# A fused attention and gated feed-forward kernel: another order for the first stretch, and the 1/rms of batches 2 to 7 by TensorE transposes

## The chip, the core and the metric

The kernel runs on one core of a Trainium2 chip. A core has engines that run side by side, each with its own queue of instructions: TensorE multiplies matrices (PE in the profile; PEld are its loads of the stationary operand), VectorE (DVE), ScalarE (ACT) and GpSimd (POOL) work on elements, and SyncE (SP) issues transfers. Results of TensorE go to PSUM, the other engines work on SBUF and PSUM. Engines wait for each other by semaphores. The metric is the device time of the whole kernel in microseconds (us).

## What is computed

Eight batches of 512 tokens with 8 heads of 64 features, and 32 states per head. Tokens read the states and states read the tokens by softmax attention; both results, 544 rows of 512 features per batch, go through an RMS norm and a gated feed-forward layer with 1536 hidden features.

```
scores  = x @ state.T / 8                    # per batch and head: 512 x 32
xread   = softmax(scores)  @ state           # tokens read states
sread   = softmax(scores2) @ x               # scores2 = state @ x.T / 8
rows    = concat(xread, sread), heads side by side      # (8*544, 512)
xn      = rows / sqrt(mean(rows^2) + 1e-6) * rms_g
out     = (silu(xn @ w_gate) * (xn @ w_val)) @ w_out    # 1536 hidden
```

The inputs w_gate, w_val, w_out come as 64-bit numbers and are converted on the chip.

## The kernel before

The kernel is a set of streams, Python generators that issue a few instructions and yield. A string of letters names the stream that goes on next; so it deals the order of instructions on TensorE, VectorE and ScalarE by hand, while GpSimd and the transfers follow the program. ORDER deals batch 0, the conversion of weights and the attention of batch 1; PERIOD deals one batch b from 1 to 7 with the attention of batch b+1; STATES deals the feed-forward layer of the states at the end.

```python
streams = {"a": tokens_read(0), "s": states_read(0), "A": tokens_read(1), "S": states_read(1),
           "e": exponents(), "d": values(),          # conversion: ScalarE's part, VectorE's part
           "v": ...own_weights(0, mp)...,            # state @ w, and its copies
           "h": of_batch_0(0), "t": of_batch_0(1), "u": of_batch_0(2),   # products, silu, gates
           "p": project_as_ready(banks_0), "c": projected(banks_0, store_tokens(0)),
           "w": first_of_batch(1), "k": weight_sums(), "z": keep_awake()}
with tc.manual_schedule(**by_hand):
    for stream in ORDER:
        if stream in "ck" and "s" not in seven:
            early.close()          # the room of raw weights is given back
            open_late()            # and the pools of the later batches are opened
            slot_sums(1)
        next(streams[stream])
...
for b in range(1, B):
    ...
    h, t, u = hidden_seven(S, weights_of(b), lambda b=b: tokens_of(b), False)
    p, c, k = project_seven(S, store_tokens(b))
    ...                            # "a" tokens_read(b + 1), "s" states_read(b + 1),
    ...                            # "w" first_products(b + 1, then); in the last batch
    ...                            # "a" is state_norm() and sums_of_w([0]), one step in four
    for stream in PERIOD:
        if stream in streams:
            step = next(streams[stream], done)
```

keep_awake (z) multiplies the identity by itself and its result is not used. From batch 1 on, products of two by two blocks are done with seven multiplications in place of eight: slot_sums makes sums of the attention weights (L610 to L613, GpSimd), more_of_v sums of the weights (L572 to L575, GpSimd), hidden_seven the products (L692) and gates, project_seven the projection (L854).

Attention of the tokens, with the norm (one yield is one step of the stream):

```python
def mean_root(ss, n):                      # L271: ss ** -0.5 on GpSimd
    ri = two.tile([P, NC], F32, name="ri")
    GE.tensor_tensor(out=ri[:, 0:n], in0=ss, in1=mhalf[:, 0:n], op=ALU.pow)
    return ri

def along_rows(ri, n):                     # L278: each column along all rows, to PSUM
    rp = aps.tile([P, NC, P], F32, name="at")
    for c in range(n):
        TE.transpose(out=rp[:, c, :], in_=ri[:, c:c + 1].to_broadcast([P, P]), identity=ident)
    return rp.rearrange("p c t -> p (c t)")

def rms_on_array(b, sq):                   # batches 0 and 1
    ...                                    # L348: four products with a column of ones
    VE.tensor_scalar(ss, sp, 1e-6, None, op0=ALU.add)
    yield "step"
    ri = mean_root(ss, NC)
    yield
    rp = along_rows(ri, NC)
    yield
    return rp

def rms_on_blocks(b, sq):                  # batches 2 to 7
    n = S // Ns                            # 16
    VE.transpose(out=sq[:, 1, :], in_=sq[:, 0, :])                       # L364
    yield
    part = one.tile([P, n], F32, name="part")
    VE.reduce_sum(out=part, in_=sq[:, 1, :]..., axis=AXX)                # L367
    yield
    sp = aps.tile([P, n], F32, name="at")
    TE.matmul(out=sp, lhsT=groups..., rhs=part, start=True, stop=True)   # L370
    yield
    ss = two.tile([P, n], F32, name="ssb")
    VE.tensor_scalar(ss, sp, 1e-6, None, op0=ALU.add)                    # L374
    yield "step"
    ri = two.tile([P, n], F32, name="rib")
    GE.tensor_tensor(out=ri, in0=ss, in1=mhalf, op=ALU.pow)              # L377
    yield
    rp = sq[:, 2, :]
    VE.transpose(out=rp, in_=ri.unsqueeze(2).to_broadcast([P, n, Ns]))   # L380
    yield
    return rp

def tokens_read(b):
    ...                                    # scores (L328), max, exp, sums (L337 to L412)
    VE.transpose(out=aT_s[b][:, e], in_=eS[:, e]...)                     # L414
    ...
    TE.matmul(out=reads[j]..., lhsT=packed..., rhs=aT_s[b]...)           # L421
    ...
    SE.activation(out=sq[:, i, :], in_=reads[j], func=ACTF.Square, ...)  # L428
    ...
    VE.tensor_tensor(out=sq[:, i, :], ..., op=ALU.add)                   # L431
    ...
    rp = yield from (rms_on_array if b < 2 else rms_on_blocks)(b, sq)
    VE.tensor_tensor(out=aT_s[b], in0=aT_s[b], in1=rp..., op=ALU.mult)   # L434
    yield "step"
```

Attention of the states: L447 and L450 (maximum), L454 (exponentials), then for batches 0 and 1 L464 (transposes on TensorE) and L466 (copies), for the others L472 (eB, transpose on VectorE), L475 (eB to e_d in DRAM) and L479 (e_d to e2T); L482 and L483 (sums), L490 (products with x), L498, L502, L504 (the result into xsT).

Conversion of one piece of the weights: L216, L218, L221 on ScalarE, then L242, L245, L249, L254 on VectorE. L546 is the product of states and weights, L588 the hidden product of batch 0, L598 its gates, L794 its projection. The gates of the later batches are L754, L757 and L769 on VectorE, copies L738, L741, L743 and the activation L745 on ScalarE.

The norm of the states, in the last batch:

```python
def state_norm():
    ...                                                            # L510: squares on ScalarE
    yield
    ...                                                            # L515: products with ones
    ss = two.tile([P, NT // P], F32, name="sst")
    VE.tensor_scalar(ss, sp, 1e-6, None, op0=ALU.add)              # L518
    ri = mean_root(ss, NT // P)
    yield
    rp = along_rows(ri, NT // P)
    for i in range(NI):
        VE.scalar_tensor_tensor(out=xsT[:, i, :], ...)             # L523
    sums_of_x()
    yield
```

Of the kernel before, what the change touches and what calls it, by code (L numbers as in the profile page):

```python
# [8 lines left out]
F32 = mybir.dt.float32  # L9
# [3 lines left out]
ALU = mybir.AluOpType  # L13
# [4 lines left out]
P = 128  # L18
# [1 line left out]
W_BUFS = 3  # L20

ORDER = (
    "aaaaaaaaddaaaaaaeaseeaasadsasszzzzzzzzzzzzzzssdsaaaasaeadesaeeazzsdasaaezzzzzzza"
    "deadaaaddeeazzzzsedaadszzzzzadaeedzzvvavdzzadeaAzzzzhdeeddtdAdAAhueheAeedtddphAe"
    "dvdvduvdphedeAedtdhApeehddeuAdddeAhdedvdtudvvpeAAAAdhdAAteAehuhpddephepdeAdAeApA"
    "dteedAAvvveAdpudAAephtdSdhAdphdeAueedhAdeAteudddeeSppAddAAdppAdAdevApvdveehhAdth"
    "AudhpdeddeedeAdteAupvdvdvphedAAtdShhutSAhpukSSSkkkwSwkpSkpwpSSckSScckkpcSwkkkwww"
    "w"
)

PERIOD = (
    "hhvthtaxhxthauhvuvthhtauhthxhaahtuuxxuxahuhuatthtuuhxhhuutuxhuhthhuhuttauhxthhhu"
    "ahuuuavhattuhtxuhhxhutuuauuthaaauhaxhhthtutuhuhuhuuuaptuuuhupuacpaaaaaaaapaaaapa"
    "kacaakapssaaaaaspcsspakcakkcaaucksaawwsxwxppxksssxppskkpsxskpcxsscs"
)

STATES = (
# [6 lines left out]
def kernel(  # L44
# [21 lines left out]
    VE, SE, GE, TE = nc.vector, nc.scalar, nc.gpsimd, nc.tensor  # L66

    B, H, S, D = x.shape
    Ns = state.shape[2]
    DM = H * D  # L70
    DFF = moe_w_gate.shape[1]
    NC = S // P
# [7 lines left out]
    consts = ctx.enter_context(tc.tile_pool(name="consts", bufs=1))  # L80
    one = ctx.enter_context(tc.tile_pool(name="one", bufs=1))
    two = ctx.enter_context(tc.tile_pool(name="two", bufs=2))
# [8 lines left out]
    seven = {}  # L91
# [17 lines left out]
    def load_x(b, *queues):  # L109
# [8 lines left out]
        for c in range(NC):  # L118
# [3 lines left out]

    ident = consts.tile([P, P], F32, name="ident")
    make_identity(nc, ident)
    mhalf = consts.tile([P, S // Ns], F32, name="mhalf")
    GE.memset(mhalf, -0.5)
    ones = consts.tile([P, 1], F32, name="ones")
    GE.memset(ones, 1.0)

    GE.tensor_tensor(out=consts.tile([P, NC], F32, name="first_pow"), in1=mhalf[:, 0:NC],  # L130
                     in0=ones.to_broadcast([P, NC]), op=ALU.pow)
    bounds = consts.tile([P, 2], F32, name="bounds")
    GE.memset(bounds[:, 0:1], 1151.0 + 7.5 / 16)
# [4 lines left out]
    for i in range(4):  # L138
        GE.tensor_copy(groups[:, i], ident[:, 0:Ns])
        for j in range(1, 4):  # L140
            GE.tensor_tensor(out=groups[:, i], in0=groups[:, i],
                             in1=ident[:, Ns * j:Ns * j + Ns], op=ALU.add)
# [125 lines left out]
    def mean_root(ss, n):  # L268
# [5 lines that stand above are left out]
    def along_rows(ri, n):  # L274
# [5 lines that stand above are left out]
# [80 lines left out]
    def rms_on_blocks(b, sq):  # L360


        n = S // Ns
# [3 lines that stand above are left out]
        VE.reduce_sum(out=part, in_=sq[:, 1, :].rearrange("p (k f) -> p k f", f=Ns), axis=AXX)  # L367
        yield
        sp = aps.tile([P, n], F32, name="at")
        TE.matmul(out=sp, lhsT=groups.rearrange("p i t -> p (i t)"), rhs=part,  # L370
                  start=True, stop=True)
        yield
        ss = two.tile([P, n], F32, name="ssb")
        VE.tensor_scalar(ss, sp, 1e-6, None, op0=ALU.add)  # L374
        yield "step"
        ri = two.tile([P, n], F32, name="rib")
        GE.tensor_tensor(out=ri, in0=ss, in1=mhalf, op=ALU.pow)  # L377
        yield
        rp = sq[:, 2, :]
        VE.transpose(out=rp, in_=ri.unsqueeze(2).to_broadcast([P, n, Ns]))  # L380
        yield
        return rp

# [123 lines left out]
    def state_norm():  # L507

        sq = one.tile([P, NI, NT], F32, name="sqT", tag="eS")
        SE.activation(out=sq, in_=xsT, func=ACTF.Square, scale=DM ** -0.5)  # L510
        yield
        sp = aps.tile([P, NT // P], F32, name="at")
        for r in range(NT // P):
            for i in range(NI):
                TE.matmul(out=sp[:, r:r + 1], lhsT=sq[:, i, P * r:P * r + P], rhs=ones,  # L515
                          start=(i == 0), stop=(i == NI - 1))
        ss = two.tile([P, NT // P], F32, name="sst")
        VE.tensor_scalar(ss, sp, 1e-6, None, op0=ALU.add)  # L518
        ri = mean_root(ss, NT // P)
        yield  # L520
        rp = along_rows(ri, NT // P)
        for i in range(NI):
            VE.scalar_tensor_tensor(out=xsT[:, i, :], in0=xsT[:, i, :], scalar=rms_g[:, i:i + 1],  # L523
                                    in1=rp[:, 0:NT], op0=ALU.mult, op1=ALU.mult)
        sums_of_x()
        yield
# [7 lines left out]
    def own_weights(b, mp):  # L534


        pv = []

        def products():
            w = w_sb.pop(b * (NM // 2) + mp)  # L540
            for e in range(2):
                pv.append(vps.tile([P, 4 * P], F32, name="pv") if b and mp % 2 == 0 else
                          aps.tile([P, 4 * P], F32, name="at"))
            for j in range(4):
                for e in range(2):
                    TE.matmul(out=pv[e][Ns * j:Ns * j + Ns, :],  # L546
                              lhsT=stT_g[b][D * e:D * e + D, j, :],
                              rhs=w[D * e:D * e + D, j].rearrange("p m k f -> p (m k f)"),
                              start=True, stop=True)
            fetch(b * (NM // 2) + mp + W_BUFS)  # L550
            yield

        def copies():
            v = (seven["v"] if b else v_0).tile([P, 2, 2, 2, P], F32, name="v")
            v_sb[b, mp] = v, None
            for e in range(2):
                SE.copy(v[:, e].rearrange("p m k f -> p (m k f)"), pv[e])  # L557
                yield
            if b:
                more_of_v(b, mp)  # L560
                yield

        return products(), copies()
# [42 lines left out]
    def slot_sums(b):  # L606

        tt = aT_t[b] = seven["late"].tile([P, 3, HS], F32, name="aT_t")
        b11, b12, b21, b22 = (aT_s[b][:, e, HS * i:HS * i + HS] for e in range(2) for i in range(2))
        GE.tensor_tensor(out=tt[:, 0], in0=b12, in1=b11, op=ALU.subtract)  # L610
        GE.tensor_tensor(out=tt[:, 1], in0=b22, in1=tt[:, 0], op=ALU.subtract)
        GE.tensor_tensor(out=tt[:, 2], in0=b21, in1=tt[:, 1], op=ALU.subtract)
        GE.tensor_tensor(out=b12, in0=b22, in1=b12, op=ALU.subtract)  # L613
# [56 lines left out]
    def sums_of_x():  # L670

        tt = seven["late"].tile([P, 3, HI, P], F32, name="x_t")
        b11, b12, b21, b22 = blocks_of_x()
        x_sums.extend(tt[:, i] for i in range(3))
        for to, a, b in ((tt[:, 0], b12, b11), (tt[:, 1], b22, tt[:, 0]), (tt[:, 2], b21, tt[:, 1]),
                         (b12, b22, b12)):
            VE.tensor_tensor(out=to, in0=a, in1=b, op=ALU.subtract)
# [138 lines left out]
    def open_late():  # L816
        seven["late"] = ctx.enter_context(tc.tile_pool(name="late", bufs=1))
        seven["v"] = ctx.enter_context(tc.tile_pool(name="vbufs", bufs=3))
        seven["vs"] = ctx.enter_context(tc.tile_pool(name="sums", bufs=3))
        seven["c22"] = ctx.enter_context(tc.tile_pool(name="late2", bufs=2))  # L820
        seven["pool"] = ctx.enter_context(tc.tile_pool(name="halves", bufs=7))
        seven["t"] = seven["late"].tile([P, 3, HM, HD], F32, name="wt")
        seven["s"] = seven["late"].tile([P, HM, HS], F32, name="hs")
# [123 lines left out]
            yield  # L947

    def first_of_batch(b):
        for mp in range(2):  # L950
            for part in own_weights(b, mp):
                yield from part

    def first_products(b, own):
        slot_sums(b)
        yield
        for part in own:
            yield from part[0]
# [15 lines left out]
    for k in range(1, RAW_AHEAD):  # L974
# [6 lines left out]
               "h": of_batch_0(0), "t": of_batch_0(1), "u": of_batch_0(2),  # L981
               "p": project_as_ready(banks_0), "c": projected(banks_0, store_tokens(0)),
               "w": first_of_batch(1), "k": weight_sums(), "z": keep_awake()}
    by_hand = dict(engines={mybir.EngineType.PE, mybir.EngineType.DVE,
                            mybir.EngineType.Activation})
    with tc.manual_schedule(**by_hand):
        for stream in ORDER:
            if stream in "ck" and "s" not in seven:
                early.close()
                open_late()  # L990
                slot_sums(1)
            next(streams[stream])
    assert all(next(stream, done) is done for name, stream in streams.items() if name != "z")
    load_state(2)
# [2 lines left out]
    for b in range(1, B):  # L997
# [11 lines left out]
        if b + 1 < B:  # L1009
            streams.update(a=tokens_read(b + 1), s=states_read(b + 1),  # L1010
                           w=first_products(b + 1, then))
# [9 lines left out]
    n = B * (NM // 2)  # L1021
# [37 lines left out]
```

## Time and profile before

| | before |
|---|---|
| time, median of 3 | 789.96 us (788.03 to 791.89) |
| span of the profiled run | 786.2 us, granted clock 0.998 |
| PE busy | 764.7 us |
| DVE busy | 540.6 us |
| ACT busy | 325.0 us |
| POOL busy | 179.6 us |

The page of a profile gives busy times of each engine, the span in 40 slices with the busy share in tenths, the chain of work that ended last, and groups of instructions by line. Further views give the waits (engine and line, for whom, us in total, times, longest), and the timeline (start in us, duration in us, engine, line, operation, output<-inputs, count; in brackets the idle time before it and who ended it). A multiplication of this kernel's 32-bit numbers shows as two records of PE, a transpose as one. The end of a PE record is modelled and overlaps the start of the next, so durations of PE add up to more than its time.

The stretches of the span: the first stretch to about 134 us, batches 1 to 7 of about 84 us each but the last, in which no attention is left, and the states' layer, whose first products begin at 711 us among the last of batch 7.

### The profile page before, as it was taken

The numbers are of one execution on the slowest core, as the hardware profiler recorded it, in microseconds if no ns is written. First come the engines' busy times: TensorE is split into PE (matmuls) and PEld (weight loads), VectorE is DVE, ScalarE is ACT, GpSimd is POOL, SyncE is SP. The second block draws the span as 40 slices with busy tenths as digits, with TensorE's granted clock in tenths as the row PEclk, the third lists the DMA queues.
The fourth block names the chain that finished last, engine by engine and source line by source line (L and its number), as shares of the span: only waits on it lengthen the run. The fifth ranks groups of instructions, "written<-read, shape, count | busy, mean of one in ns | idle before, by whom it ended". The sixth has DMA issues, their size and how long they took to land.

```text
span 786.2 us, 12078 instructions
## 1 busy us (share of the span) xinstructions
PE 764.7 (97%) x4698; PEld 583.2 (74%) x4698; DVE 540.6 (69%) x834; ACT 325.0 (41%) x536; POOL 179.6 (23%) x232
## 2 busy tenths in 40 slices
PE   6999999999999998999999999999999997999998
PEld 5643444778868876877877877788788775888997
DVE  4999997688548971888278845895379715862461
ACT  5998874652235322543154224522353223510320
POOL 2100003430424024310542052304331152300000
PEclk9999999999999999999999999999999999999999
DMA  9778864760457034720665065704451253101310
GB/s 295 222 274 311 277 188 157 253 181 3 177 167 248 1 103 151 261 80 18 207 211 158 5 201 163 226 1 161 145 188 44 75 171 130 54 1 41 122 55 27
DMA packets 73689, 112.98 MB, mean 144 GB/s; under 512 B 40865, under 2 KB 51617, under 8 KB 66721
## 3 DMA queue, kind: packets, MB, share of 16 engines
q1 hardware_dynamic: 60512, 92.75, 35.5%
q10 hardware_dynamic: 13120, 19.47, 8.4%
q8 instruction: 37, 0.61, 0.3%
q14 instruction: 20, 0.16, 0.1%
HBM read 87.56 MB, written 24.64 MB: 143 GB/s over the span
## 4 chain that ended last, share of the span: by engine, by line
PE 82%; DMA 8%; DVE 8%; issue 1%; ACTq 1%; ACT 0%; SPq 0%
PE f L692 37%; PE f L854 27%; DMA e_d<-eB 5%; PE f L794 5%; PE pv L588 4%; PE at L546 3%; DMA e2T<-e_d 2%; PE pv L546 2%; PE at L328 1%; DVE ex L249 1%; PE at L490 1%; PE at L421 1%; DVE raw L245 1%; ACTq L479 1%; DVE eB L472 1%
## 5 line engine op out<-in xcount | busy, mean ns | idle before, releaser
L854 PE MATMUL f<-wo,hb 128*128 128x256 f32 x540 | 123.9, 382 | 0.0
L692 PE MATMUL f<-aT_s,v 128*128 128x256 f32 x504 | 120.7, 382 | 1.0 <-DVE hb L769 1.0
L854 PEld LDWEIGHTS f<-wo,hb 128*128 128x128 f32 x540 | 101.5, 190 | 23.1 <-issue 9.9
L692 PEld LDWEIGHTS f<-aT_s,v 128*128 128x128 f32 x504 | 94.0, 190 | 24.7 <-issue 12.4
L692 PE MATMUL f<-aT_t,vs 128*128 128x256 f32 x336 | 87.8, 384 | 0.0
L754 DVE TENSOR_TENSOR g<-g,f 128x512 f32<-128x512 f32 (+1 forms) x96 | 61.3, 651 | 33.9 <-PE f L692 26.1
L745 ACT ACTIVATE hb<-g 128x1024 f32<-128x1024 f32 (+1 forms) x48 | 48.2, 1004 | 86.5 <-DVE g L754 86.5
L854 PE MATMUL f<-wt,hs 128*128 128x256 f32 x360 | 80.4, 379 | 0.0
L692 PEld LDWEIGHTS f<-aT_t,vs 128*128 128x128 f32 x336 | 62.6, 190 | 20.4 <-issue 11.7
L572 POOL TENSOR_TENSOR vs<-v 128x256 f32<-128x256 f32 x42 | 32.8, 780 | 188.2 <-ACT v L557 188.2
L854 PEld LDWEIGHTS f<-wt,hs 128*128 128x128 f32 x360 | 68.3, 190 | 9.4 <-issue 0.2
L891 ACT COPY ot<-f 128x256 f32<-128x256 f32 x60 | 20.8, 374 | 129.1 <-PE f L854 129.1
L377 POOL TENSOR_TENSOR rib<-ssb,mhalf 128x16 f32<-128x16 f32 x6 | 19.7, 3289 | 177.2 <-DVE ssb L374 177.2
L757 DVE SCALAR_TENSOR_TENSOR hb<-hb,g 128x1024 f32<-128x1024 f32 x42 | 54.8, 1305 | 5.1 <-ACT hb L745 5.1
L899 DVE TENSOR_TENSOR ot<-ot,f 128x256 f32<-128x256 f32 x45 | 17.4, 414 | 58.7 <-PE f L854 54.3
L557 ACT COPY v<-at 128x512 f32<-128x512 f32 x54 | 29.1, 593 | 56.0 <-POOL vs L575 31.1
L692 PE MATMUL f<-aT_t,v 128*128 128x256 f32 x168 | 43.3, 380 | 3.1 <-DVE c L754 3.1
L794 PE MATMUL f<-wo,hb 128*128 128x512 f32 x96 | 44.7, 600 | 0.0
L588 PE MATMUL pv<-aT_s,v 128*128 128x512 f32 x96 | 43.6, 593 | 0.0
L692 PE MATMUL f<-aT_s,vs 128*128 128x256 f32 x168 | 43.1, 379 | 0.0
L854 PE MATMUL f<-wt,hb 128*128 128x256 f32 x180 | 41.8, 383 | 0.0
L743 ACT COPY g<-f 128x512 f32<-128x512 f32 (+1 forms) x48 | 27.0, 562 | 34.3 <-PE f L692 34.3
(145 smaller groups left out, 1255.5 us busy)
## 6 DMA issues: line engine op xcount, KB each, us to landing
w_m<-w_d SPq DMA_DIRECT2D x48, 1024.0 KB, 5.4
out_dram<-ot SPq DMA_DIRECT2D x56, 128.0 KB, 1.8
raw<-in_moe_w_val_dram SPq DMA_DIRECT2D x6, 1024.0 KB, 5.2
raw<-in_moe_w_out_dram SPq DMA_DIRECT2D x6, 1024.0 KB, 7.8
x_b<-in_x_dram SPq DMA_DIRECT2D x96, 64.0 KB, 2.4
w_d<-w_m SPq DMA_DIRECT2D x6, 1024.0 KB, 4.9
x_d<-xB ACTq DMA_DIRECT2D x6, 1024.0 KB, 7.9
xG<-x_d ACTq DMA_DIRECT2D x24, 256.0 KB, 4.9
```

Source lines behind the costliest of these rows:

```text
L546: TE.matmul(out=pv[e][Ns * j:Ns * j + Ns, :], lhsT=stT_g[b][D * e:D * e + D, j, :], rhs=w[D * e:D * e + D, j].rearrange("p m k f -> p (m k ...
L557: SE.copy(v[:, e].rearrange("p m k f -> p (m k f)"), pv[e])
L572: GE.tensor_tensor(out=vs[:, 0], in0=a21, in1=a22, op=ALU.add)
L588: TE.matmul(out=to[0], lhsT=lhs(i, k), rhs=r, start=(i == 0), stop=(i == len(rhs) - 1))
L692: TE.matmul(out=ps[:, i, 0:half], lhsT=l[:, i, :], rhs=r, start=(start and i == 0 and k == 0), stop=(k == len(lhs) - 1), skip_group_check= ...
L743: SE.copy(gates(q)[1], q["x"][:, :, 0:half])
L745: SE.activation(out=hb[:, 2 * mp:2 * mp + 2, 0:n].rearrange("p m (c t) -> p m c t", c=2), in_=q["g"][:, :, :, 0:half], func=ACTF.Silu if s ...
L754: VE.tensor_tensor(out=to, in0=to, in1=q[ps][:, :, 0:half], op=ALU.add)
L757: VE.scalar_tensor_tensor(out=h, in0=h, scalar=1.0, op0=ALU.add, op1=ALU.mult, in1=q["g"].rearrange("p m c t -> p m (c t)"))
L794: TE.matmul(out=banks[r], lhsT=hb[:, m, P * r:P * r + P], rhs=wo[:, m, :], start=(m == 0), stop=(m == NM - 1))
L854: TE.matmul(out=banks[name][:, r, :], lhsT=lhs(k)[:, P * r:P * r + P], rhs=rhs(k), start=(start and r == 0 and k == 0), stop=(k == HM - 1) ...
L891: SE.copy(to, banks[name][:, r, :])
```

## The change

Four things differ. ORDER is dealt anew, by a longer search. The slot sums of batch 1 become the first step of stream w, which now may be the one that opens the later pools, so they come after the change of room. In batches 2 to 7 the row of 1/rms comes by a power of 4 columns and four transposes on TensorE, as in batches 0 and 1, and no longer by a power of 16 columns and a transpose on VectorE; PERIOD is dealt for that. The norm of the states gets two more yields. It is meant to fill the first stretch better. Line numbers after the change are two or three higher than before (L588 becomes L590, L692 L694, L546 L548).

```diff
 ORDER = (
-    "aaaaaaaaddaaaaaaeaseeaasadsasszzzzzzzzzzzzzzssdsaaaasaeadesaeeazzsdasaaezzzzzzza"
-    "deadaaaddeeazzzzsedaadszzzzzadaeedzzvvavdzzadeaAzzzzhdeeddtdAdAAhueheAeedtddphAe"
     ... (four more lines cut)
+    "aaaaaadaaaaadeeaaeaaeadaaaeeaaaeaaadaadeaaeadddzzzzzzzzzzzzzzzzzzzzzzzzaaadaddee"
+    "daaaeazzzzzzzzzzzvvzaddeadvazzzAeeadeaedzzzhtdddAehAuAhdAeAeeAAtdpdddedpddvvvhue"
     ... (four more lines cut)
 )
 PERIOD = (
     ... (its three lines are replaced; the counts of each letter stay)
 )
@@
-    mhalf = consts.tile([P, S // Ns], F32, name="mhalf")
+    mhalf = consts.tile([P, NC], F32, name="mhalf")
@@ rms_on_blocks
-        ss = two.tile([P, n], F32, name="ssb")
-        VE.tensor_scalar(ss, sp, 1e-6, None, op0=ALU.add)
+        ss = two.tile([P, NC], F32, name="ss")
+        for g in range(4):
+            VE.tensor_scalar(ss[Ns * g:Ns * g + Ns], sp[Ns * g:Ns * g + Ns, g::4], 1e-6, None,
+                             op0=ALU.add)
         yield "step"
-        ri = two.tile([P, n], F32, name="rib")
-        GE.tensor_tensor(out=ri, in0=ss, in1=mhalf, op=ALU.pow)
-        yield
-        rp = sq[:, 2, :]
-        VE.transpose(out=rp, in_=ri.unsqueeze(2).to_broadcast([P, n, Ns]))
+        ri = mean_root(ss, NC)
+        yield
+        rp = along_rows(ri, NC)
         yield
         return rp
@@ state_norm
                 TE.matmul(out=sp[:, r:r + 1], lhsT=sq[:, i, P * r:P * r + P], rhs=ones,
                           start=(i == 0), stop=(i == NI - 1))
+        yield
         ss = two.tile([P, NT // P], F32, name="sst")
         VE.tensor_scalar(ss, sp, 1e-6, None, op0=ALU.add)
         ri = mean_root(ss, NT // P)
         yield
         rp = along_rows(ri, NT // P)
+        yield
         for i in range(NI):
@@ first_of_batch
+        slot_sums(b)
+        yield
         for mp in range(2):
@@
-            if stream in "ck" and "s" not in seven:
+            if stream in "ckw" and "s" not in seven:
                 early.close()
                 open_late()
-                slot_sums(1)
             next(streams[stream])
```

Letters in ORDER: z goes from 40 to 42, w from 8 to 9, all others keep their counts. In the old ORDER stream s (batch 0's states) runs early, between the fillers z; in the new one it comes while batch 0's products run.

## The prediction

> **What bounds the kernel now.** I read the page first, then the waits, then the timeline of single engines.
>
> ```profile
> PE 764.7 (97%) x4698; PEld 583.2 (74%) x4698; DVE 540.6 (69%) x834; ACT 325.0 (41%) x536; POOL 179.6 (23%) x232
> ...
> PE   6999999999999998999999999999999997999998
> DVE  4999997688548971888278845895379715862461
> ...
> PE 82%; DMA 8%; DVE 8%; issue 1%; ACTq 1%; ACT 0%; SPq 0%
> ```
>
> PE is the bound nearly everywhere, so the kernel gets shorter only where PE gets less to do or waits less. What the 97% hides is seen in start times: in steady work a 128x256 record starts 0.216 us after the one before it (four L692 records take 0.86 us), though its mean duration is 382 ns. So I count PE's work from start to start.
>
> Three places are not full of useful work. First, the start:
>
> ```profile
> 11.23 6.31 PE L945 MATMUL f<-ident 128*128 128x256 f32 x28
> 17.38 1.04 PE L464 MATMUL at<-ident,e 128*128 128x128 f32 x8
> ...
> 19.21 1.10 PE L490 MATMUL at<-x_b,e2T 128*32 128x64 f32 x64
> 20.24 3.29 PE L945 MATMUL f<-ident 128*128 128x256 f32 x14
> ...
> 38.48 1.88 PE L588 MATMUL pv<-aT_s,v 128*128 128x512 f32 x4
> ```
>
> L945 multiplies the identity only to keep PE busy. The real products begin at 38.48, once DVE has scaled batch 0's weights (L434, 36.84 to 38.06). Second and third, the waits of PE and one of DVE:
>
> ```profile
> PE at L490 <- DMA e2T<-e_d: 5.2, 5, 2.0
> ...
> PE f L692 <- DVE c L754: 3.1, 1, 3.1
> ...
> DVE sst L518 <- PE at L515: 7.9, 1, 7.9
> ```
>
> In six batches PE waits for the transfer of e2T; the start times give 1.29, 2.17, 0.35, 1.05, 0.89 and 0.60 us lost, 6.35 us in all. (The view counts less because the modelled end of the matmul before reaches into the gap.) The other two belong to one event in the last batch: DVE stands 7.9 us at L518, where the norm of the states waits for PE, and the gates behind it come late. Start to start PE loses 0.46 us at L515, then 1.13 and 3.23 us: 4.8 us.
>
> **What the Trainium skill says.** "TensorE: Matmul & The Clock Gate", section "Step-by-step: what each phase is for": matmuls stay in program order, only weight loads are pulled ahead. So a matmul placed before its data is ready stops all behind it; the trace agrees, the 3.07 us wait for L754 is followed by products that were ready. Same page, "Part 4: PE-mode transpose": a full 128x128 transpose, to PSUM only, about 275 ns in a kernel. The trace has 278 ns for L278, but 109 ns from start to start, which is what I charge. "DMA: Bandwidth & Descriptors", "Anatomy of one DMA": about 2 us are fixed, mostly the receipt of the last write. The trace has 3.0 us for 128 KB of e2T and 7.8 us for the 512 KB of e_d, so there something more than the fixed part is paid. "ScalarE: Activation LUTs", "What ACT_TABLE_LOAD costs": 1283 ns for a load plus a drain; the trace has 1283 ns for each of its six loads.
>
> **The change, part by part**, with the instruction order of the changed kernel (built, not run) beside this trace.
>
> *Start.* The new order takes batch 0's states (stream s) out of the start; the tokens and the conversions before L434 stay. Off DVE's queue go L447 twice (0.61 and 0.59 us to the next start), L450 (0.07), L482 (0.20), L483 (0.09), L498 twice (0.30), L504 (0.20): 2.06 us. L434 also waited 0.75 us for the transposes, which stood behind four stretched filler records; the new order has three small fillers there. But the additions L431 now come behind the whole second weight piece and would end at about 30.0 against 30.5; then L242 and L245 (1.8 us), L352, the power on POOL (1.16 and 1.99 us in the trace) and the transposes give L434 a start near 34.5. So the first real product comes at about 36.1, 2.4 us sooner. The other side: L464 (8 x 0.109), L490 (1.03) and L502 (0.11), which replaced fillers for nothing, now stand in full PE time: 2.0 us. Net -0.4. In the full stretch DVE is as tight as PE: adding the measured starts for the new queues, the conversions for weight pairs 1 to 4 end 0.6 to 1.1 us before PE asks for them (pair 5: about nothing). ACT gets 3 us of batch 0's states and two more table loads (eight in place of six). I add 1.5 us of waits there.
>
> *Batches 2 to 7.* Where one 16-column power (3289 ns) and a DVE transpose of 711 ns made the row of 1/rms, there are now four small DVE additions, a power of 4 columns (mean 1575 ns), and four transposes on PE: 4 x 0.109 = 0.44 us, six times: +2.6 us of PE work. What DVE saves (711 ns less about 0.3) is beside PE's work and counts nothing.
>
> The period is also in another order, which matters more. Now:
>
> ```profile
> 372.95 1.19 SPq L169 DMA_DIRECT2D w_m<-w_d  x2
> ...
> 373.43 1.23 DVE L472 STREAM_TRANSPOSE eB<-e 128x1024 f32<-128x1024 f32 x1
> ...
> 374.70 0.35 ACTq L475 DMA_DIRECT2D e_d<-eB  x1
> ...
> 382.52 1.28 ACTq L479 DMA_DIRECT2D e2T<-e_d  x3
> ...
> 387.02 1.10 PE L490 MATMUL at<-x_b,e2T 128*32 128x64 f32 x64 [0.19 <-issue]
> ```
>
> e_d is sent 12.3 us before L490 starts, right behind 2 MB of weights, and takes 7.8 us. In the new order L472 stands before the squares and their sums, some 13 us ahead of L490 by the sum of PE's work, and the first two weight products of the next batch, whose ends start those 2 MB, come after L490. Both help. I take away 5.5 of the 6.35 us. A new tight place: between L370 and the transposes L278 stand six products of the old half (12 records, 2.6 us), and the chain needs 0.33 (L370 to DVE) + 0.45 (four additions) + 1.6 (power) + 0.2 (two handovers) = 2.6 us. Zero to 0.4 us may be lost each time: +1.0 us.
>
> *Last batch.* New yields part the sum of the squares from what waits for it. In the new order L519 follows the first block's activation, its product L515 stands only two records behind one that DVE needs anyway, and the scaling of the states comes after the sixth block. I take away 4 of the 4.8 us.
>
> *Batch 1's slot sums* move behind the opening of the later pools, on POOL, which the trace shows idle 79.8 us before that batch's power: nothing.
>
> Sum: -0.4 + 1.5 + 2.6 - 5.5 + 1.0 - 4.0 = -4.8 us, from 789.96 to about 785.
>
> **The rivals.** (1) *The added transposes and the moved states are all that counts*, because the waits only move: L490 no longer waits for e2T, but L278 before it waits for POOL, and a block waits elsewhere. For it: the chain to L278 has no slack by my sum, and a power took 1.99 us once. Against it: the e2T waits differ from batch to batch (0.35 to 2.17 us), which speaks for traffic, not for a fixed chain. Then +4.6 of work, less 2.4 at the start and some 4 for the last batch: about 788, or 792 with 0.7 us lost at each L278. (2) *DVE and ACT bound the first stretch.* For it: DVE is busy 14.8 of 15 us from 45 to 105, and its total work there is unchanged, so an earlier start of PE is given back while PE waits for conversions. ACT, with the added loads, would hold them further. Then the first stretch is 2 to 4 us longer than I say: 787 to 789. (3) *All waits vanish and nothing new comes*: -0.4 + 2.6 - 6.35 - 4.8 = -9, 781.
>
> **Range and chances.** The three lie between 781 and 792, mine at 785. The three times before spread by 3.9 us, so I take 778 to 792. 2% is 15.8 us: all that I found on PE to win, 2.4 + 6.35 + 4.8, is 13.6 before the added work is paid, so faster by 2% needs something that I don't see: 0.04. Slower by 2% needs a stall of some 3 us in every batch: 0.03. Within: 0.93.
>
> **What would show it.** First L590 near 36 us and first L694 (the old L692) near 134. PE's wait for e2T under 1 us in all; L278 x34 on PE; a wait of PE for POOL's ri under 0.4 us each. No wait of several us at L519, and PE's wait for L756 gone from the last batch. The distance from one L490 to the next, now 83.4 to 85.2 us, near 83.6. I am wrong if PE stands at L548 in the first stretch for more than 2 us, or if a period is over 84.5.

## The result, and the profile after

The changed kernel takes 779.01 us (median; 778.11 to 779.55), the kernel before 789.47 us on the same chip (788.03 to 791.89): a ratio of 0.9863, 95% interval 0.9836 to 0.9891. The profiled span is 776.3 us against 786.2. The prediction said 785, 4.8 us less; 10.5 us came by the medians, 9.9 by the profiled spans.

The page of the changed kernel, with the lines that answer to those shown of before: busy time by engine, and the chain that ended last by engine.

```profile
PE 764.7 (98%) x4726; PEld 586.1 (75%) x4726; DVE 538.0 (69%) x846; ACT 328.0 (42%) x538; POOL 162.8 (21%) x232
...
PE 96%; DVE 2%; DMA 0%; POOL 0%; ACT 0%; issue 0%; SPq 0%
```

PE's busy sum is the same to a tenth, with 28 records more. The chain tells more: DVE and DMA, 8% each before, are all but gone. The view of PE's waits is now this, complete:

```profile
PE at L289 <- DMA rows<-in_state_dram: 5.8, 1, 5.8
PE at L278 <- POOL ri L271: 1.3, 1, 1.3
PE at L328 <- ACT xT L302: 0.7, 1, 0.7
PE at L548 <- DVE w_m L254: 0.2, 1, 0.2
```

All four lie ahead of the first real product (36.03 us); after it the view shows no wait of PE. One batch in the timeline (start, duration, engine, operation):

```profile
364.84 1.25 DVE L472 STREAM_TRANSPOSE eB<-e 128x1024 f32<-128x1024 f32 x1
...
366.92 0.35 ACTq L475 DMA_DIRECT2D e_d<-eB  x1
...
376.74 1.02 POOL L271 TENSOR_TENSOR ri<-ss,mhalf 128x4 f32<-128x4 f32 x1 [38.90 <-DVE ss L375]
...
378.48 0.60 PE L278 MATMUL at<-ident,ri 128*128 128x128 f32 x4
...
379.01 1.10 PE L490 MATMUL at<-x_b,e2T 128*32 128x64 f32 x64
...
382.12 0.90 SPq L169 DMA_DIRECT2D w_m<-w_d  x2
```

e_d is sent 12.1 us ahead of L490, hardly other than before (12.3), but the 2 MB of weights (L169) now follow L490; e_d lands in a median of 2.6 us in place of 7.8 (KB each, median us; before, then after):

```profile
e_d<-eB ACTq DMA_DIRECT2D x6, 512.0 KB, 7.8
```

```profile
e_d<-eB ACTq DMA_DIRECT2D x6, 512.0 KB, 2.6
```

The power ends at 377.76, 0.7 us before L278. From one L490 to the next it is 83.47 us in every batch from the third on. In the last batch the norm of the states passes without a stop:

```profile
645.00 1.84 PE L515 MATMUL at<-ones,sqT 128*128 128x1 f32 x16
...
646.88 0.16 DVE L519 TENSOR_SCALAR sst<-at 128x2 f32<-128x2 f32 x1
```

### The profile page after: what moved, and what is told of

Its sections match the earlier page's. It is cut to its first block, busy times and chain, and to the rows that moved or that the text cites. A ratio compares the mean times of both kernels' runs of the same rounds, so it can differ in the third digit from the quotient of the medians.

```text
span 776.3 us, 12116 instructions
## 1 busy us (share of the span) xinstructions
PE 764.7 (98%) x4726; PEld 586.1 (75%) x4726; DVE 538.0 (69%) x846; ACT 328.0 (42%) x538; POOL 162.8 (21%) x232
## 4 chain that ended last, share of the span: by engine, by line
PE 96%; DVE 2%; DMA 0%; POOL 0%; ACT 0%; issue 0%; SPq 0%
PE f L694 38%; PE f L856 36%; PE f L796 5%; PE pv L590 5%; PE at L548 3%; PE pv L548 3%; PE at L328 1%; PE at L490 1%; PE at L421 1%; PE at L300 1%; PE at L278 1%; DMA rows<-in_state_dram 0%; DVE raw L245 0%; DVE w_m L254 0%; DVE ex L249 0%; POOL ri L271 0%
## 5 line engine op out<-in xcount | busy, mean ns | idle before, releaser
L694 PE MATMUL f<-aT_s,v 128*128 128x256 f32 x504 | 119.7, 382 | 0.0
L694 PEld LDWEIGHTS f<-aT_s,v 128*128 128x128 f32 x504 | 93.5, 190 | 25.0 <-DVE c L756 5.9
L694 PE MATMUL f<-aT_t,vs 128*128 128x256 f32 x336 | 87.0, 381 | 0.0
L271 POOL TENSOR_TENSOR ri<-ss,mhalf 128x4 f32<-128x4 f32 x8 | 9.1, 1132 | 349.6 <-DVE ss L375 233.5
L694 PEld LDWEIGHTS f<-aT_t,vs 128*128 128x128 f32 x336 | 63.2, 190 | 14.1 <-issue 5.0
L574 POOL TENSOR_TENSOR vs<-v 128x256 f32<-128x256 f32 x42 | 30.7, 731 | 137.5 <-ACT v L559 137.5
L559 ACT COPY v<-pv 128x512 f32<-128x512 f32 x42 | 22.7, 594 | 71.2 <-PE pv L548 71.2
L590 PE MATMUL pv<-aT_s,v 128*128 128x512 f32 x96 | 44.2, 597 | 0.0
L694 PE MATMUL f<-aT_s,vs 128*128 128x256 f32 x168 | 43.1, 379 | 0.0
L694 PE MATMUL f<-aT_t,v 128*128 128x256 f32 x168 | 43.1, 379 | 0.0
L856 PE MATMUL f<-wo,hs 128*128 128x256 f32 x180 | 41.5, 382 | 0.0
```

The costliest lines, as they stand in the source:

```text
L574: GE.tensor_tensor(out=vs[:, 0], in0=a21, in1=a22, op=ALU.add)
L590: TE.matmul(out=to[0], lhsT=lhs(i, k), rhs=r, start=(i == 0), stop=(i == len(rhs) - 1))
L694: TE.matmul(out=ps[:, i, 0:half], lhsT=l[:, i, :], rhs=r, start=(start and i == 0 and k == 0), stop=(k == len(lhs) - 1), skip_group_check= ...
L856: TE.matmul(out=banks[name][:, r, :], lhsT=lhs(k)[:, P * r:P * r + P], rhs=rhs(k), start=(start and r == 0 and k == 0), stop=(k == HM - 1) ...
```

## The experiments

All ratios are to the kernel before, run on the same chip. "Period" is the distance between two L490.

| run | median us | ratio, 95% interval | span us | period us |
|---|---|---|---|---|
| e1_old_first | 779.56 | 0.9872, 0.9842 to 0.9902 | 776.8 | 83.47 |
| e2_old_rms | 785.17 | 0.9941, 0.9918 to 0.9964 | 782.1 | 84.45 |
| e8_old_rms_sr_first | 775.72 | 0.9821, 0.9805 to 0.9837 | 773.8 | 83.04 |
| e9_rms_alone | 810.98 | 1.0269, 1.0249 to 1.0289 | 808.7 | 87.1 to 88.3 |
| e4_early_copy | 787.10 | 0.9971, 0.9956 to 0.9987 | 785.3 | 83.82 |
| e5_copies_ahead | 813.73 (one run) | | 811.9 | 86.9 to 90.5 |
| e3a_one_yield | 787.55 | 0.9977, 0.9957 to 0.9997 | 786.5 | 83.4 to 85.2 |
| e7_no_yields | 779.91 | 0.9875, 0.9859 to 0.9890 | 777.9 | 83.48 |
| e10_power_beside_dve | 780.11 | 0.9885, 0.9847 to 0.9923 | 778.4 | 83.59 |
| e11_changed_again | 779.51 | 0.9873, 0.9839 to 0.9907 | 777.8 | 83.47 |

### The first stretch: e1_old_first

```diff
 ORDER = (            # changed kernel, with the string of before
-    "aaaaaadaaaaadeeaaeaaeadaaaeeaaaeaaadaadeaaeadddzzzzzz...
+    "aaaaaaaaddaaaaaaeaseeaasadsasszzzzzzzzzzzzzzssdsaaaas...
@@ the slot sums of batch 1 back where open_late() is called
```

> The changed kernel with the old order of the first stretch put back (batch 0, conversions, batch 1's attention, and batch 1's slot sums where they were); the period, the yields and the rms of batches 2 to 7 stay new. My theory (the new first stretch nets about 1.5 us: 2.45 sooner at the start, about 1 of waits no longer paid, 2.0 paid for moved states): span about 777.8 against 776.3, median about 780.6, first L590 near 38.5. Rival A (DVE and ACT bound the first stretch, an earlier start is given back): no difference, 779. Rival B (the first stretch is most of the gain): 786 to 788.

Measured: span 776.8 against 776.3, medians 0.5 us apart. My 1.5 us was too much, rival B is out, and the new first stretch, the moved slot sums included, is worth some half a microsecond, less than these runs separate. The old order starts its real products at 37.54 in this run, 1.5 us later and not 2.45, and loses 0.98 us (start to start) at one point:

```profile
PE at L548 <- DVE w_m L254: 0.9, 1, 0.9
```

Against these 2.5 us stand the 2.0 us of moved states: 0.5 us. The changed kernel's trace has the states' cost directly: from start to start, L464 takes 0.44 us at 82.24 and again at 89.55, and L490 1.03 us at 98.16, 1.9 us without L502. Rival A's number nearly came, but not for its reason: DVE holds the new order nowhere, which has no wait at all from the first real product on.

Why does the same order start at 38.48 in the profile of before? In the table by stretches (us, PE, PEld, DVE, ACT, POOL busy with counts, PEclk, DMA share, GB/s) that execution and e1 have

```profile
33.00:35.00 2.00, 2.00 (x18) 0.63 (x3) 1.97 (x3) 1.63 (x3) 1.58 (x1) 0.50 1.04 328
```

```profile
33.00:35.00 2.00, 2.00 (x21) 0.80 (x7) 2.00 (x2) 1.97 (x4) 1.83 (x1) 1.00 1.10 373
```

The kernel before has half the clock there, third number from the end: L546 and the filler behind it took longer, and the transposes for L434 came late. 0.9 us of the 2.45 are this one execution, and no work of the order.

### The rms: e2_old_rms, e9_rms_alone, e8_old_rms_sr_first

e2 puts the old rms into the changed kernel:

```diff
     ... (tiles and yields cut)
-        for g in range(4):
-            VE.tensor_scalar(ss[Ns * g:Ns * g + Ns], sp[Ns * g:Ns * g + Ns, g::4], 1e-6, None,
-                             op0=ALU.add)
+        VE.tensor_scalar(ss, sp, 1e-6, None, op0=ALU.add)
-        ri = mean_root(ss, NC)             # power of 4 columns
+        GE.tensor_tensor(out=ri, in0=ss, in1=mhalf, op=ALU.pow)      # 16 columns
-        rp = along_rows(ri, NC)            # four transposes on PE
+        VE.transpose(out=rp, in_=ri.unsqueeze(2).to_broadcast([P, n, Ns]))
```

> The changed kernel with the old rms for batches 2 to 7 (one power of 16 columns and a DVE transpose in place of four additions, a power of 4 columns and four transposes on PE); new orders and yields stay. My theory (the change's gain comes from the orders and yields; the four transposes are pure PE work): 6 x 4 x 0.109 = 2.6 us less, span 773.7, median about 776.4, distance between two L490 83.03. Rival (the new period needs the short chain: with a power of 3.29 us plus a DVE transpose the weights of the slot sums come late): PE waits for aT_t or for the row of 1/rms 1 to 2 us in each of six batches, median 780 to 790.

My theory fell: 782.1 in place of 773.7, period 84.45. The rival had the direction, but not the place. The timeline:

```profile
382.08 1.21 DVE L434 TENSOR_TENSOR aT_s<-aT_s,sq 128x1024 f32<-128x1024 f32 x1
...
383.20 0.47 DVE L498 TENSOR_SCALAR sr<-at,z 128x64 f32<-128x64 f32 x2
...
383.82 1.09 PE L548 MATMUL at<-w_m,stT_g 64*32 64x512 f32 x14 [0.38 <-DVE sr L498]
```

L498 scales the result of L490, which was complete about 381.6, and with that frees the PSUM buffer that L548 writes. It stands in DVE's queue behind L434, and L434 behind the row of 1/rms, which the long power delays. PE loses 0.42 + 0.96 = 1.38 us start to start, less 0.43 for the transposes that are gone: +0.95 in each period. The long power hurts through the order of DVE's queue, not through the weights that it makes.

e9 is the other single part: the new rms in the kernel before, by the same lines the other way round.

> The kernel before with the new rms alone (four additions, a power of 4 columns, four transposes on PE); orders and yields are the old ones. Step of the prediction (the transposes are plain added PE work): 6 x 0.44 = 2.6 us more, span 788.8, median about 792. Theory now (the transposes stand ahead of L490 in PE's order, where PE waits for e2T anyway, so the wait shrinks by what is added, except where it was shorter than 0.44): about +0.2 us, median 789 to 790, e2T waits about 0.4 us shorter each. Third way (the shorter chain was itself a limit in the old order): faster than before.

All three ways failed: 21 us slower. In the old order nothing stands on PE between L370 and L278:

```profile
290.19 0.29 PE L370 MATMUL at<-part,groups 128*128 128x16 f32 x2
...
291.26 1.52 POOL L271 TENSOR_TENSOR ri<-ss,mhalf 128x4 f32<-128x4 f32 x1 [30.02 <-DVE ss L375]
...
292.84 0.65 PE L278 MATMUL at<-ident,ri 128*128 128x128 f32 x4 [2.37 <-POOL ri L271]
```

So PE stands for the whole chain, 2.65 us from L370 to L278. And the stop costs twice. The table by stretches around the same place of the batch before:

```profile
204.00:206.00 2.00, 0.98 (x12) 0.64 (x20) 2.00 (x3) 0.00 (x0) 0.97 (x1) 0.88 0.00 0
206.00:207.00 1.00, 1.00 (x16) 0.17 (x1) 0.97 (x2) 0.00 (x0) 0.00 (x0) 0.50 0.00 0
```

The granted clock falls to 0.50 behind the stop and stays there to about 208.9, in four of the six batches. There PE loses 1.6 to 2.1 us more behind the stop; in the other two it loses 1.0, waiting at L546 while DVE finishes a late L434: 1.53 in the mean. The mean period is 87.8 against 84.2 before, 3.6 more. From start to start that is 2.44 (the stop: 2.66 us from L370 to L278, where the kernel before has 0.22 from L370 to its next product) + 0.58 (the transposes, to the product behind them) + 1.53 (slow clock and L546) - 0.97 (no wait for e2T any more) = 3.58.

So the parts aren't additive. The new rms alone costs 22.5 us of span; the new orders with the old rms (e2) bring 4.1; together they bring 9.9. The new rms needs the six products that the new PERIOD puts between L370 and L278, and the new PERIOD, as it is dealt, needs the short chain.

Must it be so? e8 takes e2 and lets L490 and L498 go ahead of L434:

```diff
-    "...aaaapssssaaaaksapkakasswwwxxpxkxxpccssx"     # end of PERIOD
+    "...aaaapssssaaaaksapkassakwwwxxpxkxxpccssx"     # two turns of s ahead of a's last, which is L434
```

> The changed kernel with the old rms (as in e2_old_rms) and with one more move of letters: L490 and the scaling of its result (L498) come ahead of the scaling of the weights by the row of 1/rms (L434). My theory (e2_old_rms is slow only because L498, which PE's third L548 needs, stands on DVE behind L434, and L434 behind the long power: 1.38 us of wait each batch): the wait goes, no transposes are paid, distance between two L490 83.0 to 83.2, span about 774, median about 776.5, below the changed kernel's 779. Rival (the long chain then binds one step further on, at the slot sums on POOL and the first products that read them): distance 83.5 or more, no gain, 779 to 785.

It came as expected, in span (773.8), period (83.04) and median (775.72). The same lines as in e2:

```profile
379.09 0.44 DVE L498 TENSOR_SCALAR sr<-at,z 128x64 f32<-128x64 f32 x2
...
379.44 1.22 DVE L434 TENSOR_TENSOR aT_s<-aT_s,sq 128x1024 f32<-128x1024 f32 x1
...
379.75 1.06 PE L548 MATMUL at<-w_m,stT_g 64*32 64x512 f32 x16
```

L498 comes first, L548 follows without a wait. This version beats both kernels; e11, the changed kernel once more, gives the comparison:

> The changed kernel itself, so that it and e8_old_rms_sr_first each have an interval against the kernel before from five rounds. If e8_old_rms_sr_first is faster by the six times 0.43 us of transposes: a ratio of 0.985 to 0.987 here against its 0.982, and a span of 776.3.

Measured 0.9873 (0.9839 to 0.9907) against 0.9821 (0.9805 to 0.9837). Its period is 83.47 again, but its span 777.8, not 776.3; the 1.5 us lie ahead of the first real product (37.50 against 36.03), as told at "Left open".

### The transfer of e2T: e4_early_copy, e5_copies_ahead

e4 moves two letters in the period of the kernel before: L472 and e_d come sooner, ahead of the weights.

```diff
 PERIOD (of the kernel before)
-    "kacaakapssaaaaaspcsspakcakkcaaucksaawwsx...
+    "kacaakapssaaaaaspcsspssakcakkcaauckaawwxwx...
```

> The kernel before with only two letters of its period moved: the transposition eB (L472) and the store e_d stand earlier, behind the exponents L454 and ahead of the 2 MB of weights that are asked for next; nothing else. My theory (traffic and lead: e_d took 7.8 us because 2 MB of weights were in front of it): e_d lands in 2.6 to 3.5 us, PE's waits at L490 (6.35 us in six batches) go, median about 783. Rival (the wait is of a fixed chain, or the weights now hit e2T in place of e_d): half of it or more stays, 786 to 789.

The waits at L490 are gone, but 787.1 us came, not 783: the rival's number, but only half its reason, for the weights do hit e2T, yet PE doesn't wait for it. The landing times (KB each, median us) show the traffic theory half right:

```profile
e_d<-eB ACTq DMA_DIRECT2D x6, 512.0 KB, 2.7
e2T<-e_d ACTq DMA_DIRECT2D x24, 128.0 KB, 9.0
```

e_d is fast now, but e2T, 3.0 us before, takes 9.0: the 2 MB stand ahead of it instead. The two together take 11.7 us, more than before (10.8). What removed PE's wait is the lead: e_d is sent at 369.42 and L490 starts at 385.79, 16.4 us in place of 12.3. And the gain was given back elsewhere:

```profile
368.15 1.25 DVE L472 STREAM_TRANSPOSE eB<-e 128x1024 f32<-128x1024 f32 x1 [1.65 <-ACT e L454]
369.31 0.65 DVE L367 TENSOR_REDUCE part<-sq 128x16 f32<-128x512 f32 x1
...
370.11 0.37 PE L370 MATMUL at<-part,groups 128*128 128x16 f32 x2
```

L472 now stands ahead of L367, whose sums PE needs for L370. PE loses 0.24 us there and 0.43 at the L546 behind it, so the period is 83.82, where the order before has 83.15 without its waits: 0.67 x 6 = 4.0 us. Won were 5.8: with no wait L490 starts 0.31 us after the record before it, not the 0.22 from which the prediction counted its 6.35.

e5 is the direct test: traffic put in front of e_d in the changed kernel.

```diff
+            for k in range(2):
+                nc.scalar.dma_start(out=idle_d[b, k], in_=w_d[k])     # 1 MB each, not used
             nc.scalar.dma_start(out=e_d[b % 2]..., in_=eB...)
```

> The changed kernel with two needless copies of 1 MB each (weights to an unused place in memory) put on ACT's queue straight ahead of each e_d; nothing else moved. Theory (e_d was slow before because of 2 MB of transfers in front of it): e_d lands in 6 to 9 us in place of 2.6, e2T about 4 to 6 us later, so that its 4.6 us of room ahead of L490 are used up: PE waits there 0 to 2 us in each batch, span 776 to 785. Rival (the transfer's length is its own): e_d stays at 2.6 us, span 776.3.

```profile
e_d<-eB ACTq DMA_DIRECT2D x6, 512.0 KB, 9.3
```

```profile
PE at L494 <- DMA e2T<-e_d: 24.7, 6, 5.2
```

The landing time is as the theory has it: 512 KB behind 2 MB take 9.3 us in place of 2.6. The cost is larger than I said: PE waits 24.7 us in six batches at L490 (line 494 in this run), and the clock falls to 0.50 behind five of these stops, so the span is 811.9. The copies share a queue with e_d, which the weights before didn't, so this run is harsher than the old order was.

### The last batch: e3a_one_yield, e7_no_yields

e3a gives the kernel before the first of the two yields:

```diff
                           start=(i == 0), stop=(i == NI - 1))
+        yield
         ss = two.tile([P, NT // P], F32, name="sst")
```

> The kernel before with only the first of the two yields, the one ahead of the sum of squares of the states (L518); the DVE loop behind it (L523) still comes with it in one piece. If what costs in the last batch is DVE standing at L518 for PE's L515: the whole 4.8 us come back, 784.7. If the loop behind it (3.4 us of DVE work between two blocks) costs by itself: only the first 1.6 us or so come back, about 788, and PE still waits about 3.2 us for the gate behind it.

The median, 787.55 (1.5 us below the kernel before), is the second number, but not for its reason: from the last L490 to the last record it is 141.4 us against 143.7, so 2.3 of the 4.8 us came back. The profiled span didn't gain, as other losses differed by as much: one wait of 0.8 us at 164, some 0.5 ahead of 134, and 1.6 us behind the wait for e2T at 302, where the clock fell to 0.50 (304.68 to 308.09). The waits of 1.1 and 3.2 us for the gates are gone; in their place PE stands 0.45 + 1.45 us at L547, for the loop that scales the states (L524) and is still dealt in one piece.

e7 takes both yields out of the changed kernel:

```diff
-        yield
         ss = two.tile([P, NT // P], F32, name="sst")
@@
         rp = along_rows(ri, NT // P)
-        yield
         for i in range(NI):
```

> The changed kernel without the two yields in the norm of the states, orders as in the changed kernel. My theory (the yields remove the last batch's wait): DVE stands again at the sum of squares for PE, PE loses 3 to 5 us there, median about 783. Rival (the new period alone places L515 so that the yields no longer matter): no difference, 779.

```profile
646.89 0.16 DVE L518 TENSOR_SCALAR sst<-at 128x2 f32<-128x2 f32 x1 [1.85 <-PE at L515]
```

Between theory and rival: 1.6 us of span are lost, not 3 to 5 (the medians alone, 779.91 against 779.01 and 779.51, wouldn't tell it from nothing). DVE stands 1.85 us for L515, not 7.9, because the new PERIOD has L515 at 645 and not at 656. So in the new order about two thirds of the last batch's 4.8 us come from where PERIOD puts L515, one third from the yields.

### The chain to L278: e10_power_beside_dve

```diff
                              op0=ALU.add)
+        for i in range(2):          # not used
+            VE.tensor_tensor(out=sq[:, 2 + i, :], in0=sq[:, 0, :], in1=sq[:, 1, :], op=ALU.add)
         yield "step"
         ri = mean_root(ss, NC)
```

> The changed kernel with two needless additions of 512 columns on DVE (1.4 us together, SBUF to SBUF) straight behind the four small additions L375, so that they run beside the power of 4 columns on POOL. Theory (the recorded 1.6 us for the power was a power that ran beside DVE; alone it takes 1.02 us, and this is the 0.6 us that the hedge of +1.0 us was too much): the power takes 1.5 to 2.0 us, L278 finds its ri 0 to 0.3 us late in each of six batches, span 776 to 779. Rival (1.02 us is simply what 4 columns cost here): the power stays at 1.02, no wait, span 776.3 plus nothing.

```profile
377.61 0.67 DVE L375 TENSOR_SCALAR ss<-at 32x4 f32<-32x4 f32 x4 [3.00 <-PE at L370]
378.31 1.29 DVE L378 TENSOR_TENSOR sq<-sq 128x512 f32<-128x512 f32 x2
378.36 1.52 POOL L271 TENSOR_TENSOR ri<-ss,mhalf 128x4 f32<-128x4 f32 x1 [38.90 <-DVE ss L375]
...
380.10 0.60 PE L278 MATMUL at<-ident,ri 128*128 128x128 f32 x4
```

The power takes 1.52 us, as the theory has it, and L278 is still not late: it starts 2.82 us after L370 (377.28), as in the changed kernel (2.81). The six products between them give 2.8 us of room; the chain takes 2.1 us, or 2.6 beside DVE. The 0.12 us by which the period grew come later, where DVE's additions push L498 back.

## Why the prediction was right or wrong

The time lies in the range, and the waits that were to go went. Wrong is the size, 4.8 where 10.5 came. By the terms of the sum, for the profiled pair:

| term | predicted | measured | shown by |
|---|---|---|---|
| first real product sooner | -2.4 | -2.45, of which 1.5 by the order | e1: 37.54 with the old order at full clock |
| batch 0's states in full PE time | +2.0 | +2.0 | e1, and their starts in the changed kernel |
| waits of DVE and ACT in the first stretch | +1.5 | -0.7 | no wait after; e1 has the old 1 us again |
| transposes | +2.6 | +2.5 | e8: period 83.04, span 2.5 less |
| waits for e2T | -5.5 | -6.35 | none left; six periods of e8 are 6.3 us shorter than before |
| L278 | +1.0 | 0 | no wait; e10 |
| last batch | -4.0 | -4.8 | no wait left |
| sum | -4.8 | -9.8, of which 8.9 by the change | span -9.9 |

**The steps that failed** are the three allowances. The first is "I add 1.5 us of waits there", off by 2.2 us: I summed DVE's queue against PE's requests, found 0.6 to 1.1 us of slack, and charged for it although slack is not a wait; and I left out that the old order had its own wait there (0.7 us at 59.9), which the new one doesn't. The second is L278's +1.0. I took the mean of two powers (1.16 and 1.99 us), one of which ran beside DVE's conversions; the power in this place takes 1.02. And the room I had as 2.6 us, by counting records, is 2.8. The third is the discount of 1.65 us on waits that the profile showed whole. Each allowance leaned to the same side, and they make 4.85 us of the 5.1 by which the span gained more than forecast (5.7 by the medians). Rival (3), all waits vanish and nothing new comes, was what happened. Of the signs named, one didn't come: the first L694 starts at 136.78, not near 134. It is no measure of the first stretch, for e1 has it at 134.23 and is no shorter; other work stands ahead of it in the new order.

**A right number for half a wrong reason**: the 2.4 us at the start. I read the 0.75 us for which L434 waited behind "four stretched filler records" as work of the order; it was the clock of that execution. At full clock the order brings 1.5.

**A judgement that also failed** without moving the sum: that what the rms saves on DVE and POOL "counts nothing", so that the new rms is pure cost. In this order it isn't: with the old rms it loses 5.8 us (e2). But the saving is in one place only, L498's turn on DVE, and two letters do the same without PE's 2.5 us (e8).

**The reasons that held**: the transfer of e_d is slow because of what is in front of it (e5), though e4 shows that either more lead or a free path is enough, and that removing a wait by moving one instruction can make another behind it; rival (1), waits only move, is what e4 shows for a single move, and it is not what the searched order did.

**Left open**: how far the start can be counted on. With the new order it came at 36.0 to 36.2 us in four runs and at 37.3 to 37.5 in three; with the old one at 37.5 in e1 and at 38.4 to 38.6 in four, the kernel before among them. The filler of the start, in the changed kernel and in its second run (e11):

```profile
11.23 10.63 PE L947 MATMUL f<-ident 128*128 128x256 f32 x48
```

```profile
12.40 12.07 PE L947 MATMUL f<-ident 128*128 128x256 f32 x48
```

In the second, the scores ahead of it (L328) took 1.96 us in place of 1.09 and the filler 1.4 us more, and the fixed number of filler products hands the delay on to the attention behind them in PE's queue. The cause is PE's pace at the start: in e11 filler records start 0.43 us apart up to 15.1 us and 0.22 apart from 15.5 on; in the changed kernel they start 0.22 apart from the second on. The trace's first record of a full clock stands at 15.36 in e11 and at 9.13 in the changed kernel. It stands between 8.9 and 10.2 in six of the twelve profiled executions and between 14.3 and 15.4 in the other six, and these are the ones in which the first filler starts 1 us later. Like with like, the new order starts its real products 1.5 us sooner in the first kind (36.03 against e1's 37.54) and about 1.0 in the second (37.3 to 37.5 against 38.4 to 38.6). What decides when the full clock comes isn't shown, and what the start would be with fewer fillers wasn't tried.

## What to carry to other kernels

In a kernel that is dealt by hand, a part's worth depends on the order around it: try it alone and with the order, and look for the instruction whose turn it changes before paying for a faster operation. Don't charge for slack that is small but positive; charge for a wait only where the sum of the chain, with durations from the same neighbourhood, is over the room counted in start times. When a wait is removed by an earlier turn, look at what then stands behind the moved instruction on the same engine.

## What the runs showed of the hardware that I had not expected

A power on GpSimd depends on what DVE does: 4 columns take 1.02 us in batches 2 to 7 of the changed kernel, 1.52 beside additions or subtractions with two SBUF inputs (e10, e9), 1.99 beside the conversions of weights in the kernel before. The Trainium skill, "SBUF — State Buffer", section "SBUF: two separate sides", says that a VectorE operation with two SBUF inputs and a GpSimd operation exclude each other for the whole instruction. The trace agrees that they disturb each other; in e10, though, the power grew by 0.5 us beside 1.29 us of additions, which weren't slowed themselves (0.65 us each, where L431's of the same size take 0.69 to 0.71), so a full exclusion isn't what it shows.

A short stop of PE can cost more by the clock. "TensorE: Matmul & The Clock Gate", section "What's actually happening", has half the clock after an idle window of about 3.4 us that runs free. Here 2.62 to 2.70 us from the start before a stop to the start after it were enough for 0.50 of the clock, for 3.41 us, in four of six batches of e9, and not in the other two. A wait for e2T of 2.0 us left it at 1.00 in the kernel before (L490 at 303.6) and brought it to 0.50 in e3a (L490 at 304.2). So a stop shorter than the window can do it, but not always. That the window runs free, whatever PE does, comes out of the trace's clock records: in e9 the clock falls at 205.51, 294.25, 468.33 and 557.08 us, and the distances between these are 26, 51 and 26 times 3.413 us. The stop from 465.8 to 468.2 lies in one such stretch, which ends at 468.33; the stop from 378.7 to 381.1 lies across the bound of two, at 379.58, and left the clock at 1.00. Which share of a stretch must be idle isn't measured.
